# Seventh chunk's router logits by multiply-and-sum on VectorE, that chunk routed last of its block, and rank products half a step later

## Chip, cores, metric

The kernel runs on one core of a Trainium2 chip. The metric is the device time of one execution in microseconds. Before the change it is 438.93 us, the median of three runs (437.66 to 439.19).

## What is computed

A decayed linear attention over 1536 tokens feeds a dense feed-forward layer with ELU, and that feeds a layer of eight experts in which each token takes one expert at most. The change touches the routing of the last layer. Shortened:

```python
x = attention(q, k, v, lam)                 # (1536, 512)
x = elu(x @ w_in) @ w_out                   # d_ff = 2048
out = x.copy()
do_compute = (x @ w_skip) > 0
xc = x[do_compute]
logits = xc @ w_gate                        # (., 8)
e_idx = argmax(logits, axis=1)
gate_w = softmax(logits)[range, e_idx]
for e in range(8):
    mask = e_idx == e
    y[mask] = gate_w[mask, None] * (relu(xc[mask] @ w1[e]) @ w2[e])
out[do_compute] = xc + y
```

## The kernel before

The 1536 tokens are 12 chunks of 128, in four blocks of three chunks. Each float32 product of the feed-forward layers is three products of high and low parts (`PASSES`). The loop of the second half runs over steps n; a step belongs to block n // 16 and to one sixteenth of the hidden width. In step n TensorE does the first product of step n+2 (`ff1_mm`, 12 matmuls, line 497) and then the second product of step n in three parts, one for each chunk of the block (`ff2`, 9 matmuls, line 544). ScalarE and VectorE turn the first product of step n+1 into its ELU: `ff1_max` on VectorE (line 517, tile e), `ff1_hi` on ScalarE (line 523), `ff1_lo` on VectorE (line 528, tile g). The result of a first product lies in one of two PSUM banks named h, so `ff1_mm(n+2)` can only start when line 517 has read the result of step n.

The order on every engine is written by hand. Each engine takes its instructions in the order in which the code emits them. The tables Y, A, C, D2, B and Z hold what is put into a step: Y and A stand behind `ff1_mm`, C behind `ff1_lo`, B behind the second of the three `ff2` parts and behind `ff1_act`, Z at the step's end.

Routing of a chunk c, once the chunk's output x2 is there:

- logits: for chunks 0 to 5 each of the nine columns (eight experts and the skip score) is a multiply-and-sum on VectorE (`route_dots`, line 628) against a weight row that a DMA has broadcast to all partitions (`load_col`, line 618). Chunks 6, 7 and 8 are transposed on TensorE (`route_T`, line 584), copied to SBUF by VectorE (odd chunks, line 588) or ScalarE (line 590), and multiplied on TensorE (`route_logits`, line 599);
- `route_pick` (lines 659 to 669, VectorE) finds the expert; `route_rank` (lines 682 and 685, TensorE) counts, into a PSUM bank named aux, the tokens ahead: acc, the counts of all chunks so far, times ones, and pick times a triangle; `route_slot` (lines 700 to 703) reads that count and adds pick to acc; `route_exp` (lines 709 to 713) and `route_gate` (719 to 721) make the gate; `route_out` (726 and 727) scatters the chunk's rows into the experts' buffer xe by an indirect DMA of GpSimd.

Steps 48 to 63 are the last block. In it the experts' weights are loaded too: `load_pieces` (line 212, 1 MB each, SyncE's queue) and `conv_piece` in table C (line 138 on ScalarE, line 139 on VectorE). The first of these loads is emitted in step 48 and used in step 49. At the end of a block the three chunks are written to the output (line 566, SyncE's queue). `early` (line 976) is one read of expert 0's first rows from xe, which the last block's routing uses at line 1040. A DMA that SyncE issues waits on SyncE, so what stands behind it in that queue waits too.

Of the kernel before, what the change touches and what calls it, by code (L numbers as in the profile page):

```python
# [8 lines left out]
F32 = mybir.dt.float32  # L9
# [4 lines left out]
ALU = mybir.AluOpType  # L14
AX = mybir.AxisListType

P = 128
H = 8
D = 64
DM = 512  # L20
NF = 16
NBLK = 4
CPB = 3
# [6 lines left out]
TAIL1 = 8  # L30
QUOTA = (3, 3, 3, 3, 3, 3, 3, 3, 3, 0, 1, 3, 1, 3, 2, 2, 3, 3, 3, 3, 3)
E = 8
COPIES = 6
EF = 1024
XW = DM + 2
# [26 lines left out]
def kernel(  # L62
# [11 lines left out]
    nc = tc.nc  # L74
# [8 lines left out]
    mid = mid_stack.enter_context(pool("mid"))  # L83
# [3 lines left out]
    ph = [ph_stack.enter_context(pool("ph1", side="right"))]  # L87
    wide = wff.dtype == mybir.dt.int64

    xe = dram.tile([E * NTOK, XW], F32, name="xe")  # L90
# [29 lines left out]
    mask = mid.tile([P, H, P], F32, name="mask")  # L120
    lp = mid.tile([P, 4, P], F32, name="lp")
# [99 lines left out]
    kq_t, kv_t, xT, sc_t = {}, {}, {}, {}  # L221
# [183 lines left out]
    junk = zrow.bitcast(mybir.dt.int8)  # L405
# [142 lines left out]
    x2_t = {}  # L548
    scatters = []

    def sm(shape, dt, name, bufs=2):
        return small.tile(shape, dt, tag=name, name=name, bufs=bufs)

    def evac_y(b, t, dve=None, split=False):
        c = b * CPB + t
        x2 = ph[0].tile([P, XW], F32, tag="x2", name="x2", bufs=6)
        y = y_t.pop((b, t))
        if split:
            for cs in (slice(0, 256), slice(256, DM)):
                nc.scalar.activation(out=x2[:, cs], in_=y[:, cs], func=ACTF.Copy)  # L560
        elif (t == 1) if dve is None else dve:
            nc.vector.tensor_copy(out=x2[:, 0:DM], in_=y)
        else:
            nc.scalar.activation(out=x2[:, 0:DM], in_=y, func=ACTF.Copy)
        nc.gpsimd.tensor_copy(out=x2[:, DM + 1:DM + 2], in_=gates[:, c, 1:2])
        nc.sync.dma_start(out=out[c * P:(c + 1) * P, :], in_=x2[:, 0:DM])
        x2_t[c] = x2
# [25 lines left out]
    lg_t = {}  # L593
# [27 lines left out]
    def route_dots(k):  # L621
        for _ in range(k):
# [8 lines left out]
            if c % CPB == CPB - 1:  # L631
# [4 lines left out]
                elif e >= 7:  # L636
                    load_col(1, e - 7, slot)

    def load_late(c):

        if c == CPS + CPB:
            cols.append(big(F32))
        kq_t[c] = cols[0][:, 0:1024].rearrange("p (s k i) -> p s k i", s=2, k=4)
        kv_t[c] = cols[1][:, 1024 * (c % 2):1024 * (c % 2) + 1024].rearrange("p (s d) -> p s d", s=2)
        dma_kq(c)
        if c != CPS + CPB + 1:
            dma_kv(c)
        if c == CPS + CPB:
            kv_t[c + 1] = cols[1][:, 1024 * (1 - c % 2):1024 * (1 - c % 2) + 1024].rearrange(
                "p (s d) -> p s d", s=2)  # L650
            dma_kv(c + 1)
# [92 lines left out]
    if True:  # L744
# [14 lines left out]
        for item in loads[:3]:  # L759
# [10 lines left out]
                                in_=sel[0:H].rearrange("h k (j i) -> h k j i", j=2),  # L770
# [10 lines left out]
        J = 2 * NF - TAIL1  # L781
# [109 lines left out]
        A, B, C, D2, Y, Z = {}, {}, {}, {}, {}, {}  # L891
        early = None
# [28 lines left out]
        def put(d, n, f, *a):  # L921
            d.setdefault(n, []).append((f, a))

        def put_routes(n, c0):
            for i in range(CPB):
                if c0 > CPB:
                    put(B, n + i, route_T, c0 + i)
                put(A, n + 1 + i, route_pick, c0 + i)
                put(B, n + 1 + i, route_exp, c0 + i)
                put(Z, n + 1 + i, route_rank, c0 + i)  # L930
                put(Y, n + 2 + i, route_slot, c0 + i)
                put(B, n + 2 + i, route_send, c0 + i)

        def put_chunks(n, c0):
            for c, nxt, m in ((None, c0, n), (c0, c0 + 1, n + 2), (c0 + 1, c0 + 2, n + 4),
# [17 lines left out]
        put(Z, J + 12, load_late, CPS + CPB)  # L953
        for i in (1, 2):
            put(B, 2 * NF + 5 + 2 * i, load_late, CPS + CPB + i)
        put_routes(J + 13, 0)
        put_routes(3 * NF + 1, CPB)
        put_routes(3 * NF + 4, 2 * CPB)
        for n in range(3 * NF, N):
            f = n - 3 * NF  # L960
            if f == 0:
# [9 lines left out]
        for n in range(J, N - TAIL):  # L971
            if n == 2 * NF:
                aux_tag[0] = "aux"
            if n == 3 * NF + 10:
                early = ph[0].tile([P, XW], F32, tag="x2", name="x2", bufs=6)[:, 0:DM]
                nc.sync.dma_start(out=early, in_=xe[0:P, 0:DM])
            b, f = where(n)
            ff1_elu(n + 1)
            ff1_mm(n + 2)
            for g, a in Y.pop(n, []) + A.pop(n, []):  # L980
                g(*a)
            ff1_lo(n + 1)
            for g, a in C.pop(n, []):
                g(*a)
            ff2(n, 0)
            for g, a in D2.pop(n, []):
                g(*a)
            ff2(n, 1)
            ff1_act(n + 2)
            for g, a in B.pop(n, []):  # L990
                g(*a)
            ff2(n, 2)
            for g, a in Z.pop(n, []):
                g(*a)
            if f == NF - 1:
                for t in range(CPB):
                    evac_y(b, t)
        u = [N - 3, N - 2, N - 1]
        last = [LAST * CPB + t for t in range(CPB)]
        ff1_elu(u[1])  # L1000
# [211 lines left out]
    with tc.If(over > 0):  # L1212
# [4 lines left out]
        for c in range(NCH):  # L1217
            nc.gpsimd.indirect_dma_start(
                out=slots[:, :], out_offset=bass.IndirectOffsetOnAxis(ap=idx[:, c:c + 1], axis=0),
                in_=gates[:, c, :], in_offset=None, bounds_check=E * NTOK - 1, oob_is_err=False)  # L1220
# [96 lines left out]
```

## Time and profile before

| | us |
|---|---|
| median of three runs | 438.93 |
| the profiled execution | 436.92 |
| its span, first to last instruction | 434.8 |
| TensorE matmul busy | 422.6 |
| VectorE busy | 322.1 |
| ScalarE busy | 239.0 |
| GpSimd busy | 77.8 |
| idle time of TensorE's rank products that VectorE's pick ended | 0.8 |
| idle time of VectorE that ScalarE's line 138 ended (first of its kind in the last block) | 3.8 |

The granted clock of TensorE is 0.994 over the span. Times below are from the span's start. A step n is named by the time at which its `ff1_mm` starts: step 50 at 259.19, step 51 at 263.75, step 52 at 268.07, step 53 at 272.87, step 54 at 278.79, step 55 at 284.46, step 56 at 289.67.

### The profile page before, as it was taken

Reading aid. Unit: us, or ns where it says so; the run is one execution under the profiler, and the core shown is the slowest. Engines: PE = TensorE matmul, PEld = TensorE weight load, DVE = VectorE, ACT = ScalarE, POOL = GpSimd, SP = SyncE. Lnnn points to the kernel's source line nnn. Section 1 sums busy time; section 2 is a strip of 40 time slices with the busy share of each in tenths; the row PEclk is TensorE's granted clock in tenths of the full one; section 3 lists DMA queues with packets and bytes.
Section 4 is the critical chain, followed back from the end, with each engine's and each line's share of the span. In section 5 each row is a group of like instructions: output and inputs, shape, how many; then the busy total and the mean of one; then the engine's idle time right before and its main releaser. Section 6 shows DMA issues by size and latency. Waiting matters only on the chain.

```text
span 434.8 us, 8034 instructions
## 1 busy us (share of the span) xinstructions
PE 422.6 (97%) x3086; PEld 371.1 (85%) x3086; DVE 322.1 (74%) x703; ACT 239.0 (55%) x401; POOL 77.8 (18%) x107
## 2 busy tenths in 40 slices
PE   8999999999999999999999999999999999999992
PEld 8889999889998998998788998889897888888881
DVE  6898999998324447865887758776546799999960
ACT  2675787675443334533233445656526689888830
POOL 3853000001200120003141000222004202222211
PEclk9999999999999999999999999999999999999997
DMA  8999703998002131305141255336456899999301
GB/s 303 415 416 419 286 0 106 260 114 200 1 2 75 58 126 63 123 27 192 61 159 38 72 193 194 131 123 186 142 218 233 312 330 366 400 376 365 134 3 36
DMA packets 27649, 78.92 MB, mean 182 GB/s; under 512 B 4282, under 2 KB 8378, under 8 KB 25552
## 3 DMA queue, kind: packets, MB, share of 16 engines
q1 hardware_dynamic: 26000, 75.28, 51.1%
q0 software_dynamic: 1600, 3.03, 1.8%
q8 instruction: 26, 0.43, 0.4%
q14 instruction: 23, 0.19, 0.2%
HBM read 70.02 MB, written 10.51 MB: 185 GB/s over the span
## 4 chain that ended last, share of the span: by engine, by line
PE 82%; DVE 6%; issue 4%; DMA 3%; ACT 2%; POOL 1%; SPq 0%; POOLq 0%; ACTq 0%
PE h L497 29%; PE y L544 21%; PE h L1097 8%; PE aux L544 8%; PE y L1122 6%; PE aux L284 2%; DMA big<-in_wex_dram 1%; PE y L284 1%; DVE wa L139 1%; DMA big<-in_wff_dram 1%; PE aux L1108 1%; PE aux L599 1%; DMA out_dram<-o,ix 1%; PE aux L584 1%; PE aux L1077 1%
## 5 line engine op out<-in xcount | busy, mean ns | idle before, releaser
L497 PE MATMUL h<-xT,wa 128*128 128x384 f32 x480 | 89.8, 337 | 0.0
L497 PEld LDWEIGHTS h<-xT,wa 128*128 128x128 f32 x480 | 83.6, 188 | 3.0 <-issue 0.6
L544 PE MATMUL y<-wa,g 128*128 128x512 f32 x270 | 68.1, 396 | 0.0
L523 ACT ACTIVATE g<-e 128x384 fp32r<-128x384 f32 x64 | 33.5, 523 | 47.9 <-DVE e L517 47.9
L502 ACT ACTIVATE e<-h 128x384 f32<-128x384 f32 x64 | 31.0, 485 | 50.8 <-PE h L497 48.7
L544 PEld LDWEIGHTS y<-wa,g 128*128 128x128 f32 x270 | 49.6, 188 | 9.3 <-DVE g L528 0.3
L497 PE MATMUL h<-xT,wb 128*128 128x384 f32 x288 | 54.2, 336 | 0.0
L517 DVE SCALAR_TENSOR_TENSOR e<-e,h 128x384 f32<-128x384 f32 x64 | 35.1, 549 | 24.2 <-ACT e L505 23.9
L497 PEld LDWEIGHTS h<-xT,wb 128*128 128x128 f32 x288 | 50.5, 188 | 2.5 <-issue 0.5
L528 DVE TENSOR_TENSOR g<-e,g 128x384 fp32r<-128x384 f32 x64 | 36.2, 566 | 12.7 <-ACT g L523 12.7
L544 PE MATMUL y<-wb,g 128*128 128x512 f32 x162 | 40.6, 395 | 0.0
L628 DVE CUSTOM_DVE_ANT_0 zrow<-x,big 128x512 int8<-128x512 f32 x54 | 38.2, 707 | 0.6
L1097 PE MATMUL h<-wa,xgT 128*128 128x512 f32 x144 | 36.0, 397 | 0.1
L544 PEld LDWEIGHTS y<-wb,g 128*128 128x128 f32 x162 | 29.9, 188 | 5.5
L505 ACT ACTIVATE e<-e 128x384 f32<-128x384 f32 x64 | 33.5, 524 | 1.8
L139 DVE TENSOR_TENSOR wa<-big,wa 128x1024 fp32r<-128x1024 f32 x22 | 26.7, 1240 | 7.2 <-ACT wa L138 7.0
L1097 PEld LDWEIGHTS h<-wa,xgT 128*128 128x128 f32 x144 | 26.5, 188 | 5.7 <-ACT xgT L575 0.3
L727 POOL DMA_INDIRECT xe<-x,idx x12 | 12.2, 1015 | 98.2 <-DVE s L700 43.6
L343 POOL TENSOR_TENSOR big<-big,mask 128x512 f32<-128x512 f32 x6 | 7.3, 1214 | 106.6 <-DVE g L528 64.9
L138 ACT ACTIVATE wa<-big 128x1024 fp32r<-128x1024 f32 x22 | 22.4, 1057 | 3.9 <-DMA big<-in_wex_dram 3.9
L1122 PE MATMUL y<-wa,ht 128*128 128x512 f32 x96 | 23.7, 398 | 0.0
L139 DVE TENSOR_TENSOR wa<-ahead,wa 128x1024 fp32r<-128x1024 f32 x18 | 21.7, 1250 | 2.7 <-ACT wa L138 2.5
(231 smaller groups left out, 697.7 us busy)
## 6 DMA issues: line engine op xcount, KB each, us to landing
big<-in_wex_dram SPq DMA_DIRECT2D x17, 1024.0 KB, 6.1
ahead<-in_wex_dram SPq DMA_DIRECT2D x15, 1024.0 KB, 7.0
wb<-in_wff_dram SPq DMA_DIRECT2D x10, 1024.0 KB, 14.6
big<-in_wff_dram SPq DMA_DIRECT2D x6, 1024.0 KB, 8.9
big<-in_wgt_dram SPq DMA_DIRECT2D x18, 256.0 KB, 3.3
big<-in_kq_dram SPq DMA_DIRECT2D x6, 512.0 KB, 4.4
big<-in_kv_dram SPq DMA_DIRECT2D x6, 512.0 KB, 6.3
out_dram<-x SPq DMA_DIRECT2D x12, 256.0 KB, 2.6
```

Of the source, the lines that this page charges most:

```text
L138: nc.scalar.activation(out=w[:, 0, cs], in_=src, func=ACTF.Copy)
L139: nc.vector.tensor_tensor(out=w[:, 1, cs], in0=src, in1=w[:, 0, cs].bitcast(F32), op=ALU.subtract)
L497: nc.tensor.matmul(out=h, lhsT=w[:, wi, k * P:(k + 1) * P], rhs=xT[b][:, xi, k, :], start=(j == 0), stop=(j == 11))
L502: nc.scalar.activation(out=e, in_=h_t[n], func=ACTF.Relu, scale=-1.0)
L505: nc.scalar.activation(out=e_t[n], in_=e_t[n], func=ACTF.Exp, scale=-1.0)
L517: nc.vector.scalar_tensor_tensor(out=e, in0=e, scalar=-1.0, in1=h_t.pop(n), op0=ALU.add, op1=ALU.max)
L523: nc.scalar.activation(out=g[:, 0, :], in_=e, func=ACTF.Copy)
L528: nc.vector.tensor_tensor(out=g[:, 1, :], in0=e_t.pop(n), in1=g[:, 0, :].bitcast(F32), op=ALU.subtract)
L544: nc.tensor.matmul(out=y_t[b, t], lhsT=g[:, gi, t * P:(t + 1) * P], rhs=w[:, wi, 512:1024], start=(f == 0 and i == 0), stop=(f == NF - 1 a ...
L628: nc.vector.tensor_tensor_reduce(out=junk, in0=x2_t[c][:, 0:DM], in1=cols[0][:, slot * DM:(slot + 1) * DM], scale=1.0, scalar=0.0, op0=ALU ...
L1097: nc.tensor.matmul(out=h, lhsT=xgT_t[e][:, xi, k * P:(k + 1) * P], rhs=w_t[NF + 8 * e + k][:, wi, j * 512:(j + 1) * 512], start=(i == 0), ...
L1122: nc.tensor.matmul(out=y, lhsT=ht[:, hi, k, :], rhs=w_t[NF + 8 * e + 4 + k // 2][:, wi, (k % 2) * 512:(k % 2) * 512 + 512], start=(i == 0) ...
```

## The change

Three parts. Chunk 6 gets its logits from nine multiply-and-sums on VectorE against nine weight rows that are loaded anew by nine DMAs in step 46 into space that is free by then; chunks 7 and 8 are routed in the places that chunks 6 and 7 had, and chunk 6 in step 58. `route_rank` moves from the end of a step (Z) to the next step, behind `ff1_mm` (Y), and `route_slot` from there to B of that step. `early` moves from step 58 behind the loop.

```diff
+DOTS = (0, 4, 4, 5, 6, 7, 8, 9, 9)
...
+    def load_rows():
+        t = mid.tile([P, 6, DM], F32, tag="xT", name="rows", bufs=2)
+        m = mask.rearrange("p (s k) i -> p s (k i)", s=2)
+        for e in range(E + 1):
+            rows[e] = t[:, e, :] if e < 6 else m[:, e - 6, :] if e < 8 else lp.rearrange("p k i -> p (k i)")
+            nc.sync.dma_start(out=rows[e], in_=wgt[e:e + 1, :].broadcast_to([P, DM]))
+
+    def route_dot(c, e):
+        if e == 0:
+            lg_t[c] = sm([P, E + 1], F32, "lg", 4)
+        nc.vector.tensor_tensor_reduce(
+            out=junk, in0=x2_t[c][:, 0:DM], in1=rows[e], scale=1.0,
+            scalar=0.0, op0=ALU.mult, op1=ALU.add, accum_out=lg_t[c][:, e:e + 1])
...
-        def put_routes(n, c0):
-            for i in range(CPB):
-                if c0 > CPB:
-                    put(B, n + i, route_T, c0 + i)
-                put(A, n + 1 + i, route_pick, c0 + i)
-                put(B, n + 1 + i, route_exp, c0 + i)
-                put(Z, n + 1 + i, route_rank, c0 + i)
-                put(Y, n + 2 + i, route_slot, c0 + i)
-                put(B, n + 2 + i, route_send, c0 + i)
+        def put_route(n, c, wait=1):
+            put(A, n, route_pick, c)
+            put(Y, n + wait, route_rank, c)
+            put(B, n, route_exp, c)
+            put(B, n + wait, route_slot, c)
+            put(B, n + wait, route_send, c)
...
-        put_routes(J + 13, 0)
-        put_routes(3 * NF + 1, CPB)
-        put_routes(3 * NF + 4, 2 * CPB)
+        for i in range(CPB):
+            put_route(J + 14 + i, i, 1 + (i == 2))
+        for i in range(5):
+            c = (3, 4, 5, 7, 8)[i]
+            if c > 2 * CPB:
+                put(B, 3 * NF + 1 + i, route_T, c)
+            put_route(3 * NF + 2 + i, c)
+        put(B, 3 * NF - 2, load_rows)
+        for e in range(E + 1):
+            put(B, 3 * NF + DOTS[e], route_dot, 2 * CPB, e)
+        put_route(3 * NF + DOTS[E] + 1, 2 * CPB)
...
-            if n == 3 * NF + 10:
-                early = ph[0].tile([P, XW], F32, tag="x2", name="x2", bufs=6)[:, 0:DM]
-                nc.sync.dma_start(out=early, in_=xe[0:P, 0:DM])
...
+        early = ph[0].tile([P, XW], F32, tag="x2", name="x2", bufs=6)[:, 0:DM]
+        nc.sync.dma_start(out=early, in_=xe[0:P, 0:DM])
```

Line numbers of the changed kernel are higher by 1 at the start and by 17 in the routing functions. Three places show the new order.

SyncE's queue around steps 46 to 48; in_wgt are the weight rows of the router, in_wex the experts' weights, out_dram the stores of block 2. Before:

```order
L618 DMA big<-in_wgt_dram 128x512 x6
L566 DMA out_dram<-x_2785 128x512
L566 DMA out_dram<-x_2789 128x512
L566 DMA out_dram<-x_2793 128x512
L212 DMA big<-in_wex_dram 128x2x1024 x6
```

Now:

```order
L619 DMA big<-in_wgt_dram 128x512 x5
L647 DMA rows<-in_wgt_dram 128x512 x6
L647 DMA mask<-in_wgt_dram 128x512 x2
L647 DMA lp<-in_wgt_dram 128x512
L619 DMA big<-in_wgt_dram 128x512
L567 DMA out_dram<-x_2795 128x512
L567 DMA out_dram<-x_2799 128x512
L567 DMA out_dram<-x_2803 128x512
```

Nine loads now stand ahead of the last old weight row, of the three stores and of the first expert load, which still follows the stores.

VectorE's queue from the subtraction of step 52 to the line 517 of step 53 and a little beyond; x_1907 is chunk 4, x_2795 chunk 6, t a transposed chunk. Before:

```order
L139 TENSOR_TENSOR wa<-big,wa 128x1024
L719 TENSOR_REDUCE gsum<-d 128x1
L720 TENSOR_SCALAR gsum<-gsum 128x1
L721 RECIPROCAL x_1907<-gsum 128x1
L726 TENSOR_TENSOR idx<-sl,out_of 128x1
L709 TENSOR_SCALAR out_of<-lg 128x1
L712 TENSOR_SCALAR d<-lg,mx 128x8
L517 SCALAR_TENSOR_TENSOR e<-e,h 128x384
L700 TENSOR_TENSOR s<-aux,pick 128x8
L702 TENSOR_REDUCE sl<-s 128x1
L703 TENSOR_TENSOR acc<-acc,pick 128x8
L659 TENSOR_REDUCE mx<-aux 128x1
```

Now, from the end of chunk 4's sending on:

```order
L743 TENSOR_TENSOR idx<-sl,out_of 128x1
L726 TENSOR_SCALAR out_of<-lg 128x1
L729 TENSOR_SCALAR d<-lg,mx 128x8
L589 COPY t_3054<-aux 128x512
L652 ISA zrow,lg<-x_2795,rows 128x512
L652 ISA lg 128x1
L652 ISA zrow,lg<-x_2795,rows 128x512
L652 ISA lg 128x1
L518 SCALAR_TENSOR_TENSOR e<-e,h 128x384
L676 TENSOR_REDUCE mx<-aux 128x1
```

The three slot instructions stand ahead of the gate instructions now, behind the subtraction; the copy of chunk 7's transpose and two of chunk 6's nine sums stand ahead of line 517 (518).

TensorE's queue in step 53; x_2789 is chunk 7 before, x_2803 is chunk 8 now. Before:

```order
L682 LDWEIGHTS ones
L682 MATMUL aux<-acc,ones 128x8
L685 LDWEIGHTS ustrict
L685 MATMUL aux<-pick,ustrict 128x8
L497 MATMUL h<-xT,wa 128x384 x12
L599 MATMUL aux<-wg,t_3042 128x54 x4
L544 MATMUL y<-wa,g 128x512 x6
L584 MATMUL aux<-ident,x_2789 128x128 x4
L544 MATMUL y<-wa,g 128x512 x3
```

Now:

```order
L498 MATMUL h<-xT,wa 128x384 x12
L699 LDWEIGHTS ones
L699 MATMUL aux<-acc,ones 128x8
L702 LDWEIGHTS ustrict
L702 MATMUL aux<-pick,ustrict 128x8
L600 MATMUL aux<-wg,t_3054 128x54 x4
L545 MATMUL y<-wa,g 128x512 x6
L585 MATMUL aux<-ident,x_2803 128x128 x4
L545 MATMUL y<-wa,g 128x512 x3
```

The rank pair stands behind the first product instead of ahead of it, and the step works on chunks 7 and 8 instead of 6 and 7.

## Rows read from the trace of the kernel before

**Rows 1.** Page, part 1: engine, busy us (share), instructions.

```profile
PE 422.6 (97%) x3086; PEld 371.1 (85%) x3086; DVE 322.1 (74%) x703; ACT 239.0 (55%) x401; POOL 77.8 (18%) x107
```

**Rows 2.** Timeline of TensorE, steps 57 and 58: start, us, what.

```profile
293.92 2.25 PE L497 MATMUL h<-xT,wb 128*128 128x384 f32 x12
...
298.09 2.25 PE L497 MATMUL h<-xT,wb 128*128 128x384 f32 x12
```

**Rows 3.** The same, starts of steps 53, 54 and 55.

```profile
272.87 2.34 PE L497 MATMUL h<-xT,wa 128*128 128x384 f32 x12
...
278.79 2.33 PE L497 MATMUL h<-xT,wa 128*128 128x384 f32 x12
...
284.46 2.35 PE L497 MATMUL h<-xT,wa 128*128 128x384 f32 x12
```

**Rows 4.** Timeline of TensorE, the rank pairs of chunks 1, 2, 3 and 4.

```profile
210.31 0.18 PE L682 MATMUL aux<-acc,ones 128*128 128x8 bf16 x1
210.72 0.17 PE L685 MATMUL aux<-pick,ustrict 128*128 128x8 bf16 x1 [0.22 <-DVE pick L669]
...
214.97 0.18 PE L682 MATMUL aux<-acc,ones 128*128 128x8 bf16 x1
215.55 0.17 PE L685 MATMUL aux<-pick,ustrict 128*128 128x8 bf16 x1 [0.40 <-DVE pick L669]
...
263.35 0.18 PE L682 MATMUL aux<-acc,ones 128*128 128x8 bf16 x1
263.72 0.17 PE L685 MATMUL aux<-pick,ustrict 128*128 128x8 bf16 x1 [0.20 <-DVE pick L669]
...
268.01 0.18 PE L682 MATMUL aux<-acc,ones 128*128 128x8 bf16 x1
268.05 0.17 PE L685 MATMUL aux<-pick,ustrict 128*128 128x8 bf16 x1
```

**Rows 5.** Timeline of VectorE, steps 39 and 40.

```profile
211.81 0.69 DVE L628 CUSTOM_DVE_ANT_0 zrow<-x,big 128x512 int8<-128x512 f32 x1
...
213.59 0.16 DVE L700 TENSOR_TENSOR s<-aux,pick 128x8 f32<-128x8 f32 x1
...
213.93 0.69 DVE L628 CUSTOM_DVE_ANT_0 zrow<-x,big 128x512 int8<-128x512 f32 x1
```

**Rows 6.** Timeline of VectorE, steps 49 to 54.

```profile
259.76 1.23 DVE L139 TENSOR_TENSOR wa<-big,wa 128x1024 fp32r<-128x1024 f32 x1 [3.79 <-ACT wa L138]
...
262.25 0.55 DVE L517 SCALAR_TENSOR_TENSOR e<-e,h 128x384 f32<-128x384 f32 x1
...
268.49 1.23 DVE L139 TENSOR_TENSOR wa<-big,wa 128x1024 fp32r<-128x1024 f32 x1 [0.60 <-ACT wa L138]
...
270.35 0.55 DVE L517 SCALAR_TENSOR_TENSOR e<-e,h 128x384 f32<-128x384 f32 x1
...
274.32 0.55 DVE L517 SCALAR_TENSOR_TENSOR e<-e,h 128x384 f32<-128x384 f32 x1
...
279.53 0.68 DVE L588 COPY t<-aux 128x512 f32<-128x512 f32 x1
```

**Rows 7.** Timeline of ScalarE, step 49.

```profile
258.67 1.06 ACT L138 ACTIVATE wa<-big 128x1024 fp32r<-128x1024 f32 x1 [3.29 <-DMA big<-in_wex_dram]
```

**Rows 8.** DMA rate in 40 slices of 0.2 us from 157.0: four weight rows.

```profile
GB/s 0 0 0 0 0 0 0 82 0 0 41 143 205 195 174 164 154 215 236 215 164 154 236 225 236 256 318 399 358 328 297 225 266 102 41 20 0 0 0 0
```

**Rows 9.** Windows (last three columns: clock, DMA share, GB/s): three stores; first expert load.

```profile
135.60:137.60 2.00, 2.00 (x33) 1.75 (x35) 0.14 (x1) 0.94 (x3) 0.00 (x0) 1.00 0.98 369
...
254.00:256.50 2.50, 2.50 (x15) 2.29 (x14) 1.82 (x6) 0.76 (x2) 0.00 (x0) 1.00 0.96 364
```

**Rows 10.** Timeline of SyncE's queue: weight rows in steps 46, 47; early.

```profile
244.90 4.47 SPq L618 DMA_DIRECT2D big<-in_wgt_dram  x2
...
299.96 0.34 SPq L976 DMA_DIRECT2D x<-xe  x1
```

**Rows 11.** Timeline of TensorE: the first use of early.

```profile
322.85 1.12 PE L1040 MATMUL aux<-ident,x 128*128 128x128 f32 x8
```

More of the change, by code (lines that the diff above doesn't have):

```diff
@@ L637, in route_dots @@
                     load_col(1, e - 7, slot)
+    rows = {}
+    def load_rows():
[10 more added lines that the diff above has]
+            scalar=0.0, op0=ALU.mult, op1=ALU.add, accum_out=lg_t[c][:, e:e + 1])
     def load_late(c):
```

## Prediction

> **What bounds the kernel now.** I read the page first, then TensorE's timeline in steps 38 to 60, then what ended its waits there, then VectorE, ScalarE and SyncE at those times. TensorE is busy for 97% of the span and VectorE for 74% [rows 1], so TensorE's pace sets the end and VectorE counts only where TensorE waits for it. A step without routing takes 298.09 - 293.92 = 4.17 us [rows 2]. Steps 53 and 54, each with one chunk's logits, another chunk's transposes and a rank pair, take 5.92 and 5.67 us [rows 3]. A rank pair that waits for nothing has its second matmul 0.04 us behind its first; for chunks 1, 2 and 3 the gap is 0.41, 0.58 and 0.37, and the rows name VectorE's pick as what it waited for [rows 4]. The reader should see a second thing in step 49: VectorE stands idle for 3.79 us until ScalarE's line 138 has run [rows 6], and that one waits 3.29 us for the first expert load [rows 7]. TensorE does not feel it yet: the line 517 behind it starts at 262.25 [rows 6] and takes 0.5 us, and TensorE needs its PSUM bank at 263.35 [rows 4]. That is 0.5 us of slack.
>
> **Chunk 6 off TensorE.** From rank to rank step 51 takes 268.05 - 263.72 = 4.33 us [rows 4], so a rank costs 4.33 - 4.17 = 0.16. Step 54 is 5.67 - 4.17 - 0.16 = 1.34 us of one chunk's transposes and logits. Chunk 6's are taken away: -1.34. Step 53, with chunk 6's logits, was 0.25 longer than step 54, a wait for the copy of its transpose: -0.25. The rank of chunk 3, behind the next first product, finds its pick long done (the pick came 0.33 late): -0.33. Sum -1.92. The ranks themselves are as many as before, 0.16 each, wherever they stand.
>
> **Ranks of chunks 0 to 2.** The waits of 0.37 and 0.54 go: -0.91. What is late next is acc. The rank of chunk 1 needs the counts of chunk 0, and its slot now stands in B of step 39, behind the sum at 211.81 (0.7 us with its read-out) and 0.34 us long (213.59 to 213.93) [rows 5]: done at 212.85. TensorE is there half a step behind 210.31, at 212.3 or 212.4. I count 0.55 us as the new wait. Net -0.36; the bounds are -0.91 (the slot in time) and 0.
>
> **VectorE's queue in steps 51 to 54.** Count from line 517 at 262.25 [rows 6], with loads as before. The slot of chunk 3 (0.34) used to run while VectorE waited for the third expert piece; now it stands behind that subtraction (268.49), so the line 517 at 270.35 moves to 270.7. A pass with full routing takes 274.32 - 270.35 = 3.97 [rows 6], and I add 0.25 because the pick no longer has the slot ahead of it and the subtraction comes up against ScalarE. So the copy of chunk 7 starts at 274.9 and, at 0.68 [rows 6], is there at 275.6. TensorE, without chunk 6, reaches chunk 7's logits at 263.35 + 4.33 (step 51) + 4.33 + 0.45 (step 52 with transposes; 0.45 is a third of the 1.34) + 2.09 + 0.16 (first product and rank) = 274.7. It waits 0.9 us. Two sums of chunk 6 (1.4) and another pass (about 4.2) put chunk 7's exponent on ScalarE at 281.2; the copy of chunk 8 stands behind it in ScalarE's queue, 0.7 by the VectorE row, done at 282.0. TensorE reaches chunk 8's logits 5.75 us after 275.6, at 281.35: 0.65 us more. Together +1.5. A wait of chunk 4's rank for chunk 3's slot lies inside the 0.9. The bounds are 0 (the copy is in time, as chunk 7's was) and 2.3 (both waits half as long again). Later sums fall on passes with little or no routing and I count them at nothing: in steps 55 to 57 a pass has half of the 3.97 left, and two sums (1.4) fit under 4.17. Without that cover each costs 0.7.
>
> **Nine new loads.** SyncE issues the weight row of step 46 at 244.90 [rows 10]. The nine stand right behind it and ahead of the last old row, three stores and the first expert load. I take 1.1 us from issue to data, so the stream starts at 246.0, and 14 transfers of 0.262 MB must pass. Before, the expert load's data flowed from 254.0, at 364 GB/s and a DMA share of 0.96 [rows 9]. With the queue full, as in the three stores (369 GB/s, share 0.98 [rows 9]), one takes 0.71 us: 9.9 us, to 255.9. At the mean of the only four weight rows queued together (1.05 MB in 4.6 us, 1.15 each [rows 8]) the eleven rows take 12.7 and the stores 2.1: to 260.8. The first expert load is late by 1.9 to 6.8 us. I take 2.5, since in the last microsecond of those four, when all were queued, the slices stand at 297 to 399 GB/s [rows 8], about 0.76 us each, and nine make the queue deeper than four. All of it passes on: ScalarE and VectorE already wait for that load [rows 6, 7], their instructions are in order, the line 517 behind it frees the PSUM bank for TensorE's next first product, and the count above starts at the same line 517. So TensorE stands still for about 2 us ahead of step 51. +2.5.
>
> **Counted at nothing.** The load of early waits in SyncE's queue for chunk 6's scatter, three steps (12.5 us) later than chunk 8's was; it went out at 299.96 [rows 10] and is first read at 322.85 [rows 11], so some 10 us of cover remain. The scatters change places on GpSimd with one multiplication of the attention, both small beside its 18% share [rows 1]. What stands behind the nine loads on SyncE is the stores, which nobody reads soon, and the expert load, which is priced.
>
> **Sum.** -1.92 - 0.36 + 1.5 + 2.5 = +1.7 us. The profiled execution, 436.92 with 434.8 of span, becomes 438.6; it lies 2.0 below the median of the three runs, so against 438.93 the sum is 440.6. A measurement of this kernel can tell about 0.5%, 2.2 us, from no change: the bounds are 436.7 and 441.1.
>
> **Rivals.**
> *The loads are hidden.* At the best slice of the four rows, 399 GB/s [rows 8], 14 transfers take 9.2 us and the expert load is late by 1.2. For it: the stores' steady 369 [rows 9]; against it: the mean of the four, 230 GB/s. That is 438.93 - 0.8 + 1.2 = 439.3, and 438.1 with no delay at all. The Trainium skill (DMA: Bandwidth & Descriptors, "Where 436 GB/s comes from") puts the ceiling of the sixteen ports at 435 GB/s; by that the 14 take an estimated 8.4 us and the sum is 438.5. No row here holds that rate over two microseconds.
> *The loads cost more: slower.* One mechanism at one place: the weight rows stay at the pace of the four [rows 8], because all 128 partitions read the same 2 KB. From a delay of 3.0 us on the kernel is slower by over 0.5%; at 4.7, the middle between this point and the bound, 442.8; at 6.8, 444.9.
> *All the gain arrives.* VectorE's copy and the loads are in time, and the slot of chunk 0 too: -1.92 - 0.91 = -2.8, 436.1. For it: VectorE is idle for a quarter of the span [rows 1] and a good part of step 49. Against it: the passes of steps 51 to 54 leave no idle time beyond 0.6 us [rows 6]. It is faster by over 0.5% only if no more than 0.6 us of the losses come.
>
> **How the numbers follow.** Forecast, a delay of 1.2 to 3.0: 0.33, 439.3 to 441.1. Hidden loads: 0.22, within 0.5%. Slower: 0.32. All the gain: 0.13, faster. So faster 0.13, within 0.5% 0.55, slower 0.32. The range of 436.8 to 443.6 leaves out most of the full gain (0.1) and a delay above 5.4 (0.1).
>
> **What would show it.** In the changed profile the first line 138 on ScalarE should wait about 5.8 us for its load in place of 3.29, and TensorE should have an idle gap near 2 us ahead of a first product, ended by line 518 of VectorE. The logits of chunk 7 should wait for VectorE's copy and those of chunk 8 for ScalarE's, 0.6 to 0.9 us each. The rank pairs of chunks 2 and 3 should stand 0.04 apart, and that of chunk 1 wait for chunk 0's slot. Steps 53 and 54 should lose chunk 6's 1.34 us. If the wait for the first expert load has not grown, the largest term is wrong and the time falls below 439; if the logits don't wait either, the full gain is there.

## The result, and the profile after

The changed kernel takes 442.26 us (median of six runs, 442.04 to 442.67), the kernel before beside it 439.06 (437.6 to 439.94): a ratio of 1.0079, 95% interval 1.0059 to 1.0100. It is slower by 0.8%, inside the range of the prediction (436.8 to 443.6) and 1.7 above its value. The profiled execution is one of 442.04, with a span of 439.9 (434.8 before) and a granted clock of 0.996. Page of the changed kernel, part 1, as [rows 1]:

```profile
PE 423.7 (96%) x3074; PEld 371.2 (84%) x3074; DVE 326.8 (74%) x721; ACT 238.3 (54%) x400; POOL 77.6 (18%) x107
```

TensorE has 12 matmuls less and is busy 1.1 us longer; VectorE has nine sums more. Busy shares say nothing of where 5.1 us of span went. The step starts do: read when `ff1_mm` of each step begins, and take differences.

| us | before | after | more |
|---|---|---|---|
| start of step 38 (ahead of all edits) | 200.56 | 201.32 | 0.76 |
| steps 38 to 40 | 15.02 | 14.50 | -0.52 |
| step 41 | 6.54 | 7.60 | 1.06 |
| step 42 (has chunk 2's rank now, 0.17) | 4.15 | 4.32 | 0.17 |
| step 43 | 6.38 | 7.27 | 0.89 |
| steps 44 to 49 | 26.54 | 26.67 | 0.13 |
| steps 50 to 59 | 47.23 | 49.04 | 1.81 |
| step 60 to the end of the span | 128.38 | 129.18 | 0.80 |

The first row is spread between executions: over all traces of this study step 38 starts between 200.52 and 203.21, whatever the kernel. In part it goes with TensorE's clock. In seven of the fourteen traces the granted clock is 0.89 in the mean from 10 to 25 us, because it stands at 0.50, the lower of its two levels (1.2 GHz), for a part of that stretch; in the second trace of the kernel before it fell while TensorE waited 2.31 us for GpSimd. These seven start step 38 at 201.91 to 203.21; the other seven, with 1.00 there and the first traces of before and after among them, at 200.52 to 201.93.

That second trace of the kernel before repeats steps 38 to 60 to 0.08 us (110.11 in place of 110.03). So edits are judged below by steps, and times by medians with an interval. Steps do not always repeat so well: up to step 45 run 1 and run 12 have the order of the kernel before and take 0.9 to 1.0 longer, and run 7 has that of the changed kernel and takes 0.9 less. Apart from the kernel before, each kernel's steps are those of one execution.

**The last block** waits where the forecast had it. SyncE's queue after; rows, mask and lp are the nine new loads:

```profile
247.67 2.80 SPq L647 DMA_DIRECT2D rows<-in_wgt_dram  x6
250.57 1.03 SPq L647 DMA_DIRECT2D mask<-in_wgt_dram  x2
251.65 0.56 SPq L647 DMA_DIRECT2D lp<-in_wgt_dram  x1
252.30 0.54 SPq L619 DMA_DIRECT2D big<-in_wgt_dram  x1
253.02 2.40 SPq L567 DMA_DIRECT2D out_dram<-x  x3
255.71 0.39 SPq L213 DMA_DIRECT2D big<-in_wex_dram  x1
```

ScalarE's first expert piece after, where [rows 7] had 3.29, and VectorE behind it, where [rows 6] had 3.79:

```profile
263.21 1.06 ACT L139 ACTIVATE wa<-big 128x1024 fp32r<-128x1024 f32 x1 [4.89 <-DMA big<-in_wex_dram]
```

```profile
264.30 1.23 DVE L140 TENSOR_TENSOR wa<-big,wa 128x1024 fp32r<-128x1024 f32 x1 [4.33 <-ACT wa L139]
...
266.79 0.55 DVE L518 SCALAR_TENSOR_TENSOR e<-e,h 128x384 f32<-128x384 f32 x1
```

Against the start of step 50 (261.68, before 259.19) that piece is 2.05 us later. TensorE's waits in the last block: the starts of steps 51, 53, 54 and 55 (as [rows 3]), the rank pair of chunk 4, the logits of chunks 7 and 8:

```profile
267.39 2.35 PE L498 MATMUL h<-xT,wa 128*128 128x384 f32 x12 [1.39 <-DVE e L518]
274.57 0.18 PE L699 MATMUL aux<-acc,ones 128*128 128x8 bf16 x1 [0.51 <-DVE acc L720]
277.23 2.25 PE L498 MATMUL h<-xT,wa 128*128 128x384 f32 x12
280.17 1.10 PE L600 MATMUL aux<-wg,t 128*128 128x54 f32 x8 [0.65 <-DVE t L589]
283.69 2.25 PE L498 MATMUL h<-xT,wa 128*128 128x384 f32 x12
286.53 1.10 PE L600 MATMUL aux<-wg,t 128*128 128x54 f32 x8 [0.54 <-ACT t L591]
289.59 2.25 PE L498 MATMUL h<-xT,wa 128*128 128x384 f32 x12
```

**Steps 41 and 43** were not forecast. VectorE in step 41 before (start 215.58), then after (start 215.82):

```profile
217.22 0.16 DVE L719 TENSOR_REDUCE gsum<-d 128x1 f32<-128x8 f32 x1
...
217.80 0.22 DVE L712 TENSOR_SCALAR d<-lg,mx 128x8 f32<-128x8 f32 x1
217.93 0.55 DVE L517 SCALAR_TENSOR_TENSOR e<-e,h 128x384 f32<-128x384 f32 x1
218.39 0.16 DVE L700 TENSOR_TENSOR s<-aux,pick 128x8 f32<-128x8 f32 x1
```

```profile
217.95 0.16 DVE L717 TENSOR_TENSOR s<-aux,pick 128x8 f32<-128x8 f32 x1
218.22 0.15 DVE L720 TENSOR_TENSOR acc<-acc,pick 128x8 bf16<-128x8 bf16 x1
218.29 0.15 DVE L736 TENSOR_REDUCE gsum<-d 128x1 f32<-128x8 f32 x1
...
218.87 0.22 DVE L729 TENSOR_SCALAR d<-lg,mx 128x8 f32<-128x8 f32 x1
219.00 0.54 DVE L518 SCALAR_TENSOR_TENSOR e<-e,h 128x384 f32<-128x384 f32 x1
```

The slot (line 717 now, 700 before) stands ahead of the subtraction of line 518 (517) where it stood behind it, and the whole queue lies later against TensorE, which no longer stops for the pick in step 40. Line 518 starts 3.18 us into the step in place of 2.35. Step 41 has a product of the attention whose PSUM bank line 518 frees; TensorE after:

```profile
219.60 0.27 PE L358 MATMUL h<-big 64*64 64x64 f32 x1 [0.68 <-DVE e L518]
```

In step 43 GpSimd's queue has changed. After, then before:

```profile
230.53 1.03 POOL L744 DMA_INDIRECT xe<-x,idx  x1 [1.30 <-DVE e L518]
231.57 0.19 POOL L750 COPY gates<-x 128x1 f32<-128x1 f32 x1
232.12 0.10 POOL L403 MEMSET blank<- 128x1 f32 x1 [0.36 <-PE aux L285]
```

```profile
225.38 1.20 POOL L727 DMA_INDIRECT xe<-x,idx  x1 [3.74 <-DVE e L517]
...
229.53 0.10 POOL L402 MEMSET blank<- 128x1 f32 x1 [1.64 <-PE aux L284]
```

The memset is the signal between two halves of an attention product: it waits for TensorE's first half and TensorE's second half waits for it. Chunk 2's scatter used to end almost three microseconds ahead of it; now it stands beside the attention's small matmuls. In this trace the memset is not what holds TensorE: it waits for TensorE itself (0.36), and TensorE pauses among the matmuls with no releaser that the profile shows:

```profile
231.83 0.30 PE L358 MATMUL h<-big 64*64 64x64 f32 x3 [0.39 <-issue]
```

### The profile page after: what moved, and what is told of

The parts are those of the page before. It is cut to its first block, busy times and chain, and to the rows that moved or that the text cites. A ratio compares the mean times of both kernels' runs of the same rounds, so it can differ in the third digit from the quotient of the medians.

```text
span 439.9 us, 8042 instructions
## 1 busy us (share of the span) xinstructions
PE 423.7 (96%) x3074; PEld 371.2 (84%) x3074; DVE 326.8 (74%) x721; ACT 238.3 (54%) x400; POOL 77.6 (18%) x107
## 4 chain that ended last, share of the span: by engine, by line
PE 65%; DVE 14%; DMA 9%; issue 5%; ACT 4%; SPq 1%; POOL 0%; POOLq 0%; ACTq 0%; DVEq 0%
PE h L498 21%; PE y L545 14%; PE h L1118 8%; PE aux L545 8%; PE y L1143 6%; DVE wa L140 3%; DMA big<-in_wff_dram 3%; DMA big<-in_wex_dram 3%; ACT wa L139 2%; DVE zrow L629 2%; PE aux L285 1%; DVE e L518 1%; DVE wb L140 1%; DMA rows<-in_wgt_dram 1%; DMA wb<-in_kq_dram 1%
## 5 line engine op out<-in xcount | busy, mean ns | idle before, releaser
L629 DVE CUSTOM_DVE_ANT_0 zrow<-x,big 128x512 int8<-128x512 f32 x54 | 37.3, 691 | 1.6 <-DMA big<-in_wgt_dram 1.0
```

The source lines that it names most:

```text
L629: nc.vector.tensor_tensor_reduce(out=junk, in0=x2_t[c][:, 0:DM], in1=cols[0][:, slot * DM:(slot + 1) * DM], scale=1.0, scalar=0.0, op0=ALU ...
```

## Experiments

One table for all of them: steps from the traces, the lateness of ScalarE's first expert piece (its start less that of step 50), medians, and ratios to the kernel before that was measured beside (439.06 for the change, 438.96 for runs 1 to 4, 438.35 for 5 to 8, 439.62 for 9 to 12).

| kernel | step 41 | step 43 | 38 to 45 | 50 to 59 | first piece | median | ratio (95%) |
|---|---|---|---|---|---|---|---|
| before | 6.54 | 6.38 | 42.05 | 47.23 | -0.52 | 439.06 | |
| before again | 6.52 | 6.38 | 42.07 | 47.29 | -0.47 | 440.09 (one run) | |
| after | 7.60 | 7.27 | 43.69 | 49.04 | 1.53 | 442.26 | 1.0079 (1.0059 to 1.0100) |
| 1 old ranks, chunks 0 to 2 | 7.39 | 6.39 | 42.99 | 49.64 | 1.96 | 442.08 | 1.0067 (1.0044 to 1.0090) |
| 2 later sends | 6.76 | 6.39 | 42.65 | 49.43 | 1.92 | 441.47 | 1.0060 (1.0035 to 1.0086) |
| 3 ranks alone | 7.55 | 7.26 | 43.66 | 47.56 | -0.93 | 440.20 | 1.0024 (1.0007 to 1.0042) |
| 4 one load | 7.59 | 7.24 | 43.66 | 46.41 | -1.02 | not comparable | |
| 6 slot behind | 6.49 | 6.38 | 42.31 | 48.93 | 1.32 | 442.16 | 1.0090 (1.0068 to 1.0113) |
| 7 rows in step 49 | 7.29 | 6.73 | 42.80 | 49.02 | -0.90 | 442.52 | 1.0096 (1.0072 to 1.0121) |
| 8 both | 6.49 | 6.39 | 42.27 | 49.16 | -0.68 | 441.72 | 1.0082 (1.0059 to 1.0105) |
| 9 rows between | 7.55 | 7.23 | 43.56 | 47.18 | -0.60 | 442.12 | 1.0063 (1.0041 to 1.0085) |
| 10 rows and sends | 6.48 | 6.39 | 41.65 | 47.60 | 0.04 | 439.54 | 1.0003 (0.9983 to 1.0023) |
| 11 the same, old ranks in the last block | 6.50 | 6.38 | 41.66 | 46.06 | -0.55 | 438.37 | 0.9970 (0.9954 to 0.9985) |
| 12 chunk 6 alone | 7.39 | 6.42 | 43.07 | 50.76 | 3.07 | 441.36 | 1.0044 (1.0024 to 1.0063) |

### Steps 38 to 45

**1.** Chunks 0 to 2 routed by the old rule.

```diff
+        def put_old(n, c):
+            put(A, n, route_pick, c)
+            put(B, n, route_exp, c)
+            put(Z, n, route_rank, c)
+            put(Y, n + 1, route_slot, c)
+            put(B, n + 1, route_send, c)
...
-            put_route(J + 14 + i, i, 1 + (i == 2))
+            put_old(J + 14 + i, i)
```

> The changed kernel with the routes of chunks 0 to 2 alone in their old places (rank at the end of a step, slot and scatter in the next); everything else stays. Theory (GpSimd's memset behind the scatters costs some 2.0 us in steps 41 and 43, and the later ranks give 0.5 back there): faster than the changed kernel by 1.4 to 1.6 us, about 440.7, with the span between the starts of steps 38 and 44 back at 32.1 us from 33.7. Rival (the late ranks gain 0.4 us as in the prediction and the offset of steps 41 to 43 is something that the block would show anyway): slower than the changed kernel by 0.4, 442.7.

Neither came. Step 43 is back at 6.39, as the theory had it, but step 41 takes 7.39, and the kernel is level with the changed one. The wait in step 41 has no releaser, and the scatter beside it is the next thing to see (TensorE, then GpSimd):

```profile
220.35 0.22 PE L358 MATMUL h<-big 64*64 64x64 f32 x1
220.92 0.25 PE L358 MATMUL h<-big 64*64 64x64 f32 x1 [0.35 <-issue]
```

```profile
219.59 0.98 POOL L744 DMA_INDIRECT xe<-x,idx  x1 [2.83 <-DVE d L729]
```

**5.** The kernel before once more, unchanged, for a second trace, since up to step 45 run 1 has its instructions.

> The kernel before, unchanged, for a second trace. Its first one lies 2 us below its median, and the kernel with the old ranks of chunks 0 to 2 runs the same instructions in step 41 and took 7.39 us there against 6.54. Theory A (a scatter of GpSimd beside the attention's small matmuls holds TensorE up in most executions, and the first trace happened to escape): step 41 takes 7.2 to 7.5 us here. Theory B (6.54 is what the kernel before takes, and something else in the changed kernel costs the 0.85): 6.5 to 6.6 again.

Step 41 takes 6.52: B, as far as the kernel before goes. But run 1 (and run 12, 7.39 too) has the same instructions there in the same order on every engine, so B's "something else in the changed kernel" is not in that order either. See below under what stays open.

**2.** Gate and scatter of chunks 1 and 2 a step later.

```diff
-            put(B, n + wait, route_send, c)
+            put(B, n + wait + later, route_send, c)
...
-            put_route(J + 14 + i, i, 1 + (i == 2))
+            put_route(J + 14 + i, i, 1 + (i == 2), int(i > 0))
```

> The changed kernel with the gate and scatter of chunks 1 and 2 one step later, so that each scatter stands behind that step's memset in GpSimd's queue; the ranks and slots stay half a step later. Theory (the memset behind the scatter is the whole loss there): faster than the changed kernel by 1.8 to 2.1 us, about 440.3, TensorE's second half of the attention product in steps 41 and 43 starts 0.5 us or more earlier after the first half than in the changed kernel, and the kernel is some 0.5 us faster than the one with the old ranks of these chunks. Rival (VectorE's slot and idx, not GpSimd, hold the step): no more than 0.5 us.

Steps 41 and 43 fall to 6.76 and 6.39, 1.7 us together, as expected; the kernel gains only 0.8. Part of the rest is in step 44, 6.55 in place of 5.83: chunk 2's scatter now stands ahead of that step's memset, and TensorE waits for it. Here the memset does what the theory had said of steps 41 and 43:

```profile
236.50 1.21 POOL L744 DMA_INDIRECT xe<-x,idx  x1 [3.58 <-DVE e L518]
237.72 0.20 POOL L750 COPY gates<-x 128x1 f32<-128x1 f32 x1
237.93 0.10 POOL L403 MEMSET blank<- 128x1 f32 x1
```

```profile
238.08 0.40 PE L285 MATMUL aux<-mask,state 64*64 64x64 f32 x12 [0.64 <-POOL blank L403]
```

The edit moves the gate off VectorE's queue ahead of line 518 as well, so it does not tell VectorE and GpSimd apart in step 41.

**6.** In addition chunk 1's slot behind the line 518 of step 41.

```diff
+            if c == 1:
+                put(Y, n + wait + 1, route_slot, c)
+            else:
+                put(B, n + wait, route_slot, c)
```

> The changed kernel with the scatters of chunks 1 and 2 one step later and chunk 1's slot behind the next step's subtraction of line 518, so that neither slot nor gate stands ahead of the line 518 on which step 41's attention waits. Theory (in step 41 it is VectorE's queue ahead of line 518, in step 43 the scatter beside the small matmuls): steps 41 and 43 take 6.4 to 6.6 and 6.4 us (7.60 and 7.27 in the changed kernel), 0.2 less than with the later scatters alone, and 2.0 less than the changed kernel, 440.3, less what the first expert load takes back. Rival (the memset's place in GpSimd's queue alone): as with the later scatters alone, 441.5.

Step 41 falls from 6.76 to 6.49 by the slot alone, with line 518 at 2.31 us into the step; GpSimd's queue is that of run 2. So VectorE's queue ahead of line 518 is one cause in step 41. The time did not follow (442.16), although steps 38 to 45 are 1.38 shorter than in the changed kernel; the spread ahead of step 38 and between runs (440.83 to 443.03) is as large, so the verdict here rests on the steps. Runs 8, 10 and 11 keep this slot and have 6.48 to 6.50 there.

### The nine loads

**4.** Eight of the nine loads left out; all nine sums read one row, so chunk 6's tokens all go to one expert and what follows the last block is another program. Only steps up to 60 are read.

```diff
-            rows[e] = t[:, e, :] if e < 6 else m[:, e - 6, :] if e < 8 else lp.rearrange("p k i -> p (k i)")
-            nc.sync.dma_start(out=rows[e], in_=wgt[e:e + 1, :].broadcast_to([P, DM]))
+            rows[e] = t[:, 0, :]
+        nc.sync.dma_start(out=rows[0], in_=wgt[0:1, :].broadcast_to([P, DM]))
```

> The changed kernel with one weight row loaded in place of nine; all nine sums read that one row, so the chunk's logits are all that of expert 0. Theory (nine loads ahead of the first expert load make it 2 us late and TensorE stands for it): ScalarE's first wait for an expert load falls from 4.89 to about 3.3 us, faster than the changed kernel by 1.4 to 2.1, about 440.5. Rival (VectorE's nine sums and the copies behind them bound those steps, the load being hidden behind them): under 0.5 us, 441.8 or more.

ScalarE's wait is 2.34, below that of the kernel before, step 51 starts without a wait, and steps 50 to 59 take 46.41, 2.63 less than the change and 0.82 less than before. So eight of the loads cost 2.6 us there, and without that cost the last block gains 0.8 on before, the later ranks and slots counted in.

**7.** The nine loads behind the second expert load, the sums in steps 53 to 57.

```diff
-DOTS = (0, 4, 4, 5, 6, 7, 8, 9, 9)
+DOTS = (5, 6, 6, 7, 7, 8, 8, 9, 9)
...
-        put(B, 3 * NF - 2, load_rows)
...
+                put(B, n + 1, load_rows)
```

> The changed kernel with the nine weight rows loaded in step 49, behind the second expert load in place of ahead of the first, and chunk 6's sums in steps 53 to 57 in place of 48 to 57. Theory (the nine loads cost 2.6 us where they stand): ScalarE's first wait for an expert load is about 3.3 us again, steps 50 to 60 take 46.0 to 46.8 us in place of 49.0 (47.2 before), and the kernel takes 439.4 to 440.0. Rival (the third expert load is now late by as much as the first was): its wait on ScalarE grows from nothing to 2 us or more and the time stays within 0.7 of 442.3.

The first piece is in time, and steps 50 to 59 still take 49.02: the rival. SyncE's queue shows why:

```profile
254.77 10.23 SPq L213 DMA_DIRECT2D big<-in_wex_dram  x2
265.05 3.01 SPq L647 DMA_DIRECT2D rows<-in_wgt_dram  x6
268.11 1.69 SPq L647 DMA_DIRECT2D mask<-in_wgt_dram  x2
271.04 0.33 SPq L647 DMA_DIRECT2D lp<-in_wgt_dram  x1
273.23 3.32 SPq L213 DMA_DIRECT2D big<-in_wex_dram  x2
```

The second expert load waits some 10 us for its space, the nine rows wait behind it, and the third expert load behind them: ScalarE's piece of it, at 280.86, has an idle time of 2.05 us ahead. The row of that wait names TensorE's transposes, but the DMA engines move some 400 GB/s from 271 to 281 and the load, issued at 273.23, lands 7.4 us later, its last part at 280.78, so I put it down to the load. And the sums in pairs, steps 54 to 57, are not free: steps 56 to 58 take 4.70, 4.67 and 4.58 in place of 4.17, with TensorE waiting for line 518.

This trace also tells something of steps 41 and 43. Up to step 45 the kernel has the changed kernel's order on every engine, and its scatters stand at the same places; but TensorE does not pause beside them, and the steps take 7.29 and 6.73 in place of 7.60 and 7.27. What is left over run 6 (6.49 and 6.38) has a releaser in both. In step 41 it is 0.80, with TensorE's wait for line 518 at 0.68 as in the changed kernel. In step 43 it is 0.35: the memset stands behind scatter and gate, and TensorE's second half starts at its end.

```profile
232.48 0.10 POOL L403 MEMSET blank<- 128x1 f32 x1
```

```profile
232.64 0.27 PE L285 MATMUL aux<-mask,state 64*64 64x64 f32 x1
```

**9.** The rows between the first and the second expert load, into that gap.

```diff
-DOTS = (0, 4, 4, 5, 6, 7, 8, 9, 9)
+DOTS = (4, 4, 5, 6, 7, 8, 8, 9, 9)
...
-        put(B, 3 * NF - 2, load_rows)
...
+                put(B, n, load_rows)
```

> The changed kernel with the nine weight rows issued between the first and the second expert load (the second is held 10 us by its space in the trace with the rows in step 49, so the DMA engines are idle there) and chunk 6's first sum in step 52 in place of 48. Theory (the nine loads cost 2.6 us by their place alone): the first wait of ScalarE for an expert load is 2.3 to 3.3 us, steps 50 to 60 take 46.2 to 46.9 us (49.0 in the changed kernel, 46.4 with one load), 2.2 to 2.8 us faster than the changed kernel, 439.5 to 440.1. Rival (the sums on VectorE cost as much as the loads): steps 50 to 60 at 48 or more and a gain under 1 us.

The first piece is in time and step 51 starts 4.17 after step 50: 1.86 us gained in steps 50 to 59, not 2.2 to 2.8. The kernel gains 0.16% on the changed one by the two ratios, far less: TensorE waits 0.74 us for ScalarE's g behind the last steps (0.20 in the changed kernel). I put it down to the second sum that now stands in step 56. Runs 7, 8 and 10 have the same pair there and wait 0.74 to 0.76; run 11 has the pair and waits less than 0.1, with the old ranks and slots. So the pair alone does not make the wait; with the later ranks and slots it does.

### The parts

**3.** The ranks alone: all nine chunks by the new rule, chunk 6 on TensorE, no rows and no sums, the read of early in its old place.

```diff
-            c = (3, 4, 5, 7, 8)[i]
+            c = CPB + i
...
-        put(B, 3 * NF - 2, load_rows)
...
```

> The kernel before with the ranks, slots and scatters of all nine chunks moved as in the change, and nothing else: chunk 6 stays on TensorE in its old place, no new loads. Theory: the steps 38 to 44 cost 1.6 as in the changed kernel, the last block gains the rank wait of chunk 3 and loses up to 0.7 at the copies behind the later slots: slower than before by 1.3 to 2.3 us, 440.3 to 441.4. Rival (all the loss is that of the loads and the nine sums): 438.3 to 439.1, the kernel before or a little less.

440.20, 1.24 over before: just under the theory's range, above the rival's. Its steps show the loss in full, the pauses included: 43.66 against 42.05 in steps 38 to 45, and in the last block the later rank gains 0.37 in step 50 and loses 0.66 in step 53 at a copy.

**12.** Chunk 6 alone: all ranks and slots in their old places, loads and sums as in the change.

```diff
-            put_route(3 * NF + 2 + i, c)
+            put_old(3 * NF + 2 + i, c)
...
```

> Chunk 6's part of the change alone: nine loads in step 46, nine sums, chunk 6 routed last, with all ranks and slots in their old places. Theory: steps 38 to 46 as before (42.05, or 0.9 longer where the unexplained pause of TensorE in step 41 falls), steps 50 to 60 at 48.7 to 49.3 us: slower than before by 1.8 to 2.3. With the run of the ranks alone (1.2 over before in the medians, 1.9 in the trace) the two parts add to the change's 3.2. Rival (the two parts only lose together): within 0.7 us of before.

441.36, 1.7 over before, and 1.2 + 1.7 = 2.9 against the change's 3.2: the parts add. The steps missed the expectation (50.76 for 50 to 59). In this execution, the slowest of its eleven runs, the first expert piece is 3.6 us late, and with the rank at a step's end TensorE waits for the pick behind line 518, not for line 518 alone:

```profile
269.87 0.17 PE L702 MATMUL aux<-pick,ustrict 128*128 128x8 bf16 x1 [3.76 <-DVE pick L686]
269.89 3.90 PE L498 MATMUL h<-xT,wa 128*128 128x384 f32 x12
```

Behind that wait TensorE's granted clock is 0.57 in the mean from 270 to 274 us (down to 0.50, the lower of its two levels, 1.2 GHz), in place of 1.00: the first product takes 3.90 us in place of 2.35, and step 51 5.88 in place of 4.33. That is 1.55 of the 50.76; without it the steps are 49.2, inside what was expected. It is the only trace whose clock falls between steps 38 and 60.

The lateness for the same nine loads is 1.8 to 3.6 us over five traces (runs 1, 2, 6, 12 and the change, against -0.52 before). Run 12 shows chunk 6's gain by itself as well: no copy is waited for, and steps 52 to 56, with the clock back at 1.00, take 24.06 us in place of 25.85.

### Together

**8.** Runs 6 and 7 in one.

> Both edits together: later scatters and slot of chunks 1 and 2, and the weight rows behind the second expert load. Theory (the two losses are separate and add): faster than the changed kernel by 4.0 to 4.8 us, 437.5 to 438.3, a little faster than the kernel before or level with it. Rival (the gain in steps 38 to 44 is waited out at the first expert load, as step 51 suggests): no more than 3 us off, 439.3 or more.

The rival's number (441.72), not its reason: steps 38 to 45 keep their gain (42.27), but steps 50 to 59 take 49.16, as in run 7.

**10.** Run 9 with run 6's slot, and chunk 2's scatter one more step later, behind the memset of step 44 (`put_route(J + 14 + i, i, 1 + (i == 2), i)`).

> The rows between the two expert loads, chunk 1's slot behind the next subtraction, and the scatters of chunks 1 and 2 one and two steps later, so that no scatter stands beside or ahead of a step with attention products. Theory: steps 38 to 46 take 41.6 to 41.8 us (43.7 in the changed kernel, 42.05 before), steps 50 to 60 as in the run with the rows alone, together 4.2 to 4.8 us faster than the changed kernel: 437.5 to 438.1, some 0.5 to 1.3 below the kernel before. Rival (the gain of steps 38 to 46 is given back at the first expert load): no faster than the run with the rows alone by 0.7.

Steps 38 to 45 take 41.65, 2.04 less than the change and 0.4 less than before. The time is 439.54, level with the kernel before, 1.4 above what was expected and 2.6 below run 9 beside it: the gain is carried to the end. What is missing lies in the last block, 47.60, and behind it, where TensorE waits 0.74 for ScalarE's g.

**11.** The same with the old ranks and slots in the last block (`put_old` for chunks 3 to 8).

> The same with the ranks and slots of the last block in their old places (rank at the end of a step, slot behind the next first product). Theory (there the later rank gains 0.37 at step 51 and loses 0.66 at the logits of chunk 7, as the run with the ranks alone has it): steps 50 to 60 are 0.2 to 0.5 us shorter than with the later ranks. Rival (the later ranks help there once chunk 6 is gone from TensorE): 0.3 us longer or more.

1.54 us shorter in steps 50 to 59, three times what I expected, 1.0 shorter from step 61 to the use of early (the wait for g is gone), and 1.2 us in the median: 438.37, 0.3% below the kernel before with an interval that excludes level. The traced execution is the fastest of the twelve, 2.8 below their median, so its steps are those of a good case. With the slot behind line 518 the logits of chunk 7 start without a wait and those of chunk 8 wait 0.11. SyncE's queue of this kernel, the rows in the gap:

```profile
251.85 0.39 SPq L213 DMA_DIRECT2D big<-in_wex_dram  x1
252.30 4.17 SPq L647 DMA_DIRECT2D rows<-in_wgt_dram  x6
256.57 2.08 SPq L647 DMA_DIRECT2D mask<-in_wgt_dram  x2
258.98 0.33 SPq L647 DMA_DIRECT2D lp<-in_wgt_dram  x1
262.07 11.61 SPq L213 DMA_DIRECT2D big<-in_wex_dram  x3
```

## Why the prediction was right or wrong

**The loads: right.** +2.5 was forecast, with TensorE standing still for about 2 us ahead of step 51 by line 518. The piece is 2.05 us later than before, TensorE waits 1.39, and with one load the steps are 2.63 shorter. The nine rows and what stood with them ran at 302 GB/s from 248 to 258 us, between the 230 and the 369 from which the bounds were taken. The ceiling that was cited beside the rival (435 GB/s, the Trainium skill, DMA: Bandwidth & Descriptors, "Where 436 GB/s comes from") was not held: read in stretches of two microseconds, 253 to 255 had 360 and 258 to 260, with the expert load, 417.

**VectorE's queue in steps 51 to 54: right in size and places.** +1.5 was forecast; 0.65 at chunk 7's logits by VectorE's copy, 0.54 at chunk 8's by ScalarE's and 0.51 at chunk 4's rank make 1.70. Run 11 shows the cause: with ranks and slots in their old places 0.11 of the 1.70 is left, and in run 12, with the nine loads where they were, nothing above 0.1.

**Chunk 6 off TensorE: right in size.** -1.59 was forecast without the rank of chunk 3 (1.34 and 0.25), and run 12 has -1.79 in steps 52 to 56; the rank's -0.33 is -0.37 in run 3. But steps 53 and 54 were named for it, and step 53 still has one chunk's logits and another's transposes: in run 12 it falls by 0.25, step 54 by 0.46 and step 55, which has lost its logits, by 0.96. In the last block the three terms summed to 2.1, and 1.81 was measured.

**Ranks of chunks 0 to 2: the step that failed.** The forecast was -0.36, with bounds of -0.91 and 0. What it looked at came: the rank pairs stand together, and chunk 1's waits 0.31 for acc:

```profile
213.62 0.17 PE L699 MATMUL aux<-acc,ones 128*128 128x8 bf16 x1 [0.31 <-DVE acc L720]
213.65 0.17 PE L702 MATMUL aux<-pick,ustrict 128*128 128x8 bf16 x1
```

Steps 38 to 40 gained 0.52. But the working followed the slot only to the next rank. In the last block it had counted the slot ahead of line 517; in step 41 it did not, although the attention waits there for the same line. And under "Counted at nothing" the scatters "change places on GpSimd with one multiplication of the attention, both small beside its 18% share": a share is an average, and in step 43 the scatter came ahead of the memset between the attention's matmuls. Steps 41 and 43 cost 1.95 us. Of these 1.10 have a releaser in run 7, which has the same order and no pause (0.75 by VectorE's queue ahead of line 518 in step 41, 0.35 by the memset in step 43); the other 0.85 are TensorE's pauses, whose cause stays open. Runs 6, 8, 10 and 11, with chunk 1's slot behind line 518 and no scatter beside the attention of steps 41 and 43, have 6.5 and 6.4 there again. Runs 10 and 11, with no scatter ahead of the memset of step 44 either, have the 0.4 that was forecast over steps 38 to 45 (41.65 against 42.05).

**Counted at nothing, the tail.** early was in time, as forecast. But from step 61 to its use the kernel takes 12.88 us against 12.26: chunk 6's slot and gate of step 59 put VectorE behind, and TensorE waits 0.20 for ScalarE's g among other things. The runs with old ranks in the last block (11 and 12) have 12.54 and 12.27 there.

**The sum.** The failed step (2.0) and the tail (0.6), less 0.3 in the last block, are 2.3 us beyond the forecast in the trace; the medians differ by 3.2 in place of 1.7, 1.5 beyond it. The 5.1 us of the traces hold the 0.8 ahead of all edits, so 4.3 lie behind; the execution traced of before lies 2.1 under its median and that of after 0.2, and of the 4.3 some 1.1 are not in the medians. With one trace of the change no run tells which. "Slower", at 0.32, came by a mechanism that the text did not have; the rival for it (loads at 230 GB/s) did not happen. That the time lies inside the range is luck in part: the upper end was drawn for late loads, and what came on top of the forecast came from elsewhere. One figure of the rivals is off and nothing hangs on it: the middle between delays of 3.0 and 6.8 is 4.9, 443.0 us, where 4.7 and 442.8 stand.

**What stays open.** TensorE's pauses among the 64x64 matmuls. Where a scatter runs beside them, the pause ends 1.27 to 1.33 us after the scatter's start (the change and runs 1, 3, 4, 9 and 12), and steps 41 and 43 without a scatter beside them have none. But in two traces of before a scatter stands at the same place in step 41 and there is no pause, with the order of run 1; and run 7 has none in steps 41 and 43, with the order of the change. So a scatter beside them is not enough. The Trainium skill (Perfetto Trace Analysis, "DMA Instruction — SWDGE (GPSIMD)") has the record of such a DMA end with the descriptors and not with the data, so the 0.98 to 1.03 us of the rows are no bound for what it does. The changed kernel's trace agrees: the scatters land 2.8 us after their issue in the median. In step 43, where the scatter starts at 230.53, the DMA engines move nothing from 230.5 to 232.1 (0 GB/s) and 191 GB/s from 232.1 to 232.8; the pause is over at 231.83. So neither the scatter's data nor any other transfer was moving while TensorE paused. Whether the scatter's work on GpSimd holds TensorE, and why in some traces alone, no run here tells: only the kernel before was traced twice, so the pause may go with the program as well as with the execution. It wasn't tried to take the scatters out.

## To carry over

Follow a moved instruction on its own engine to the next instruction there that someone waits for, in every step that it passes, not only to its reader. A load may be small and still cost its whole time by standing ahead of the one that is waited for: look for a gap in which the queue is held by space, and put it there. And a signal through a third engine (here a memset on GpSimd) makes that engine's queue part of the critical path however idle it is.

## Not expected of the hardware

The pauses of 0.34 to 0.39 us without a releaser among small matmuls, in 6 of the 14 traces, are the one thing; in steps 41 and 43 they were seen only beside an indirect DMA of GpSimd, before its data moved, and three traces have the DMA at the same place and no pause. The second is that the same nine loads, in the same order, made the next one late by 1.8 us in one execution (run 6) and 3.6 in another (run 12). The third is what a single wait can cost beyond its length: in run 12 TensorE stood for 3.76 us and its next product, at the lower clock, took 1.55 longer.
